# A recurrence and an FFT convolution in one kernel: filter spectra on 112 partitions, projection groups of five rows, merged products, and a new written order

## The chip, the cores and the metric

The kernel runs on one core of a Trainium2 chip. The metric is the time of one execution on the device in microseconds, given as the median of several runs. A profile is one further execution, recorded instruction by instruction; its span is the time from the program's first to its last instruction.

## The reference

Batch 4, sequence S = 6272, width D = 256. A gated recurrence runs along the sequence; its result goes through a projection into three parts, of which the second is convolved along the whole sequence with a filter (by FFT), multiplied with the other two, and projected out.

```python
sig = 1.0 / (1.0 + np.exp(-f_logit))
f = lower_bound + (1.0 - lower_bound) * sig
for t in range(S):
    h = f[:, t] * h + (1.0 - f[:, t]) * x[:, t]
    y[:, t] = h
proj = y @ w_proj                              # 256 -> 3 * 256
x1, x2, x3 = proj[..., :D], proj[..., D:2*D], proj[..., 2*D:]
X2 = np.fft.rfft(x2, n=S, axis=1)
H = np.fft.rfft(filter_fft, n=S, axis=0)
x2_conv = np.fft.irfft(X2 * H, n=S, axis=1)
out = (x1 * x2_conv * x3) @ w_out
```

## The kernel before

S is split as 128 x 49, so that the Fourier transform becomes two steps of matrix products: 128 points on the partitions (tables D1, FT) and Q = 49 rows beside them. TB = 98 partitions hold real and imaginary parts of the 49 row frequencies. The width is handled as NEP = 128 pairs of channels, in NU = 16 units of UE = 8 pairs.

- `prepare` builds the tables and the filter's spectra: it loads the filter (`ff`), turns it (`rot`, `f2`), applies the two steps (`FF1` with copies `afs`, then `FF2` with copies `hw`), and stores each pair of units into a DRAM tile H (`hst`): 128 rows, and then 64 rows once more, so that a load can read row p and row p + 49 for partition p. Tiles of H are shared by two units.
- `hgrn(b)`: 13 chunks of 512 steps. SP loads x and f_logit into XT and FL (`load`), ACT takes the sigmoid (`sig`, L324), POOL multiplies (`u`, L326), PE turns both (`su`, L338), ACT or DVE makes the gate (`f`, L351 and L353), DVE runs the scan (`scan`, L359) into HA. The first WR = 3072 steps of each half are copied behind the end (`wrap`, L367), so that strided columns can wrap around: a copy in SBUF of 512 f16 elements, given to POOL, ACT or a DMA of SP.
- `gate(b)`: x1 and x3 projections (`x13`, L387), evacuated (`xs`) and multiplied into zt (`z`, L417 on POOL, or L408 directly on DVE).
- `spectrum(b)`: `phase_p` projects x2 for all 49 rows (L705), four rows to a group of two PSUM banks, 13 groups of which the last has one row; each group is copied into X2 (`x2`, L281 or L286), every row twice, 64 columns apart. Then for each unit `phase_f1` (first step, L718, needing every group, and copy `A` into HA) and `unit` (second step F2, L777; the product with the filter's spectrum read from Hu, either directly by DVE from PSUM, L798, or copied by ACT and multiplied by POOL, L807; inverse step I2, L817, copied to Th). `spectrum_load` fetches a unit's spectrum from H into Hu. The zero-frequency column of four units at a time goes through `mini` (L734), two small DVE products (L740) and an addition on POOL (`slot`, L782).
- `phase_o(b)`: inverse step I1 (L851), product with zt (`y`, L857), output projection (`proj`, L869), copy (`o`) and store.

Matmuls, copies and DMAs are recorded as operations of a plan, each with the engines that may run it and a cost. Nothing is scheduled when the program is built: the string ORDER gives, in one written list, every operation's place, its engine and its first PSUM bank. An operation that takes `take` banks holds them until its reader is done. All four batches are interleaved in this list: while unit after unit of batch b runs, gates of b and scans of b + 1 stand between. Extra `warm` products (L591) fill PE's stream in the beginning and at the end.

SP issues all DMAs on one queue, in the list's order; a DMA whose buffer isn't free holds those behind it.

Of the kernel before, what the change touches and what calls it, by code (L numbers as in the profile page):

```python
# [11 lines left out]
F16 = mybir.dt.float16  # L12
I32 = mybir.dt.int32
AOP = mybir.AluOpType
# [9 lines left out]
M = 128  # L24
Q = 49
TB = 98
# [10 lines left out]
UE = 8  # L37
NU = NEP // UE
MARGIN = 1.0
FS = 1.0 / 8.0  # L40
HS = 64.0 / S / FS
# [4 lines left out]
NX2 = 13  # L46
# [13 lines left out]
class Plan:  # L60
# [68 lines left out]
    "YAKAEiCFCgEjKEkYEmGEnOCpQCqACwUCrYAIACjQCxME3AE4YCkAEtSAJAEuKEvKExWFLgCuUGHgEyGEzOCvECyYCsQFMgFDAFEYE5UE6ME7ME9S"
    "CtAE+CFVgE/KEwYC5WE8YC6GCzQC0AC+WFNAFFUFIQFWgFfgFggFGMC2gC/GFJIDASC3WFOYDBCFHMC4GC7YDCYFXAFYYDHSC8WFKIFPUFQMFSQF"  # L130
    "pgFqgFRMC9GDICDDWDJSFTAFUIFZUFaMDEGDKCDLYFbMDOWFhAFiYFcQFzgF0gDPGFdAFeIDQSDRCDSYDZWDMUDTSFjQDNMCGgFrAFsYAGgDaGDU"
    "CFkIFlICmgDeWDfGDXUDYEDbYF1AF2YALADgSDhKFmWF9gF+gFnOFoODcUDdEFtQFuAFvIDpSCFgFwUDnWDqCDjSFxEFyMAMAE0YDiYEEYEcYEoY"
    "DoGDrYF/AGAYF3QF4IDkCFAYDuWDvOANAMegF5IDwUDxEC1gF6SF7CF8KEAYDsWEMYJbUJcVJeNMqgDyYJgQJhRGBSDtGClgJdECVgEQYJfYJiAG"
    "CKDzWJjBJkYGDKDWgGEUD3QGIgJlSJmTGFMGGMD0GD2gGtgJnKJorGJUGKED4ADVgGPWGQOGbSGcCGdUGeMGLQGMAGRSGSKGVUGWMMgAGXQGYIGZ"
    "SGaCDFgGTWGUOCWgMsAGNUGOMGhQGiIDGgGfSGgCJqWJrXD1gJvUJxMJwQJyoJzYJsGJtHJuYGjSGkCJ0RGpUGqEJ1QJ2BJ3IJ4YGuSGwqGxYGlW"
    "GmGJ5QGnUGoEJ7IJ6RDmgG/gJ+SJ/QKACGyqGzYDlgKDWKEXKBAJ8pKFGGrSKCYG2gG3UGsKGvYG7EKGvHAQHEAHRSHSCG5sKIVJ9YG8YKKFG6YG"
    "0WHCoKJRHDYG4YHBYHFYHXSHJUHYKG1GKLBHTWHUGG9QG+AHKYHVSHWCHGWHHGKNQKORMrgMtYJpYHIgHNsHOYHLsHMYKPAKHYKQBM2gM4AHZSHa"
    "KHcUKMYHdYHlWHnGHbgMfgKRYHesHfYHgsHhYHPSHmYHQCHkgHoYHtgKSQKTRKVJKXUKUAKZMHpuHqYH/VIAFHiSHjCIDQHuUIEAHvYIBWICGHrS"
    "HsCMhYHysHzYH3QH4YIFWIGGH2gKWYHwsHxYH0UH1EIKSH5oH6YH7oH8YIJgIHWIIOIMCINYILYIOqKYQKaoKbYITUISgIPYIVEIcRIeBH9WH+GI"
    "UYIXsIbgKcUKdTKeEKfrM3gItQIuAIQWIRGIWYKhUKiVKkFIdYIfYIkgKjMI3gMiQMjAIgpIhYKlYMkIIlWIpGIYYMmUMnEMoMNDgIZSIqYImYIa"  # L140
    "CM5YKmXKoHIiQIjAInuIoYIxSIyCMuUMvMMwMIvQIwAIzWI0GKnSKrTKtDI4QKpqNCgJAgI6oI7YI1UI2MI8AI9YJJgI5YMyWNOgMzGM0OJBSJDC"
    "NPgKqYNEANFYKsRKupJSgKwQKyAIrUJEYIsEKxSJFqJGYM6WM7GKzqM+QNagNbgM8OM/ANAIKgYI+UJLYI/EJCYK1TK2SK3DK0YK4qK5YNQANGUN"
    "RYNKWNmgNngNHEK6TNIMK8DNLGJTQJXAJVANMOJHSJUYJWYJICJKUNcAK7RJMsJNYK/QK9pK+YLBAJOsJPYNSSNTCLAWNUKLCGNdYLDYKvYLEULG"
    "ENWQNwgNxgNXALFXLJWLHvJQUNYINoANpYJRELKSLOTLPXLQDLRvNBgLSYNeUNiQN7gN6gLLGNfELMqJYYNgMNjANyANzYLTTLUWLYSLaCNkILVD"
    "LWuLXYLZXLbvLcYNqUNrENsMLIYLNYNtSOEgOFgNVANuCNvKJZQNhYJaAR7WR9GMpgR8XLdQLeIR+HN0ULiSLjKN8AN9YN1EN2MN3WOOgOPgN4GN"
    "5ONNYNZALfQLgALhgLkSLnULoMLlCN+QLmgN/AOAISAWSBXSCGNlYLsSLtKSDHOGAOHYOBUOYgOZgOCEODMLxWOQAORYLpQLyOLqALrgLuSLvCLw"
    "gL2UL3MOIQOJAOKIOLWOMGONOOigOjgLzSL0COSUL7QL8IOaAObYM9YNJYL1gOVSU+gOWCOXKMlAOTEOUMMxAL4WL5GL6gU/gL9QL+AL/gOkAOlY"
    "MASMBKMFWMGOOcUOdEOeMOfQVLgVKgOgAOhIMCSMDCMEgMHWM1YOmUOnEOpSOqCOoMOrKVWgMKQMLIMPUMQMMIGMJgO6SO7KO8WO9GPCQPDAO4UO"
    "5EO+SO/KPEQVAAVXgPFAVBYO0WO1GOuUOvEOyQOzIOwSOxKVMAVNYOsUOtMVYAO2QO3IPAWPBGMMSMNCMUUMVMPKQPLIVZYPGWPHGMRSMOgMSCMZ"
    "UMaMR/YSEYPQWPUuPVYPIQPJAPMUPNEMTgPSuPTYSFSSHKSGTSIDSJYMWQPOUPPMPZYPRYMXAPYWPogPauPbYPcuPdYPpSPrCPgUPkESKQSMAPWR"  # L150
    "PhYPlYPisPjYPXBPzVP0FP7gSLQSPXSRHSNoPeRPqYPtqPuYPsYSQUSUQSWIPfBPxWPyGSVVSXtSYYSSESTYP3SP4KP1QP2APmWP8UPnGQAsQBYP"
    "vQP5SP6KQGYP9YPwAP+sP/YQFWQHGQEgQIYQJuQKYSZVQNgSbFQfQQgAQXSQOVSaUQSFSeQSgAScsSdYQbKMYgQWgQCWQPYQTYQDGQQtQRYSfRSj"
    "QShpSiYSkTSlAQpgSmDQhWQiGQLUQYYQcYSnYQZqQaYQMEQjQQkAQUWQVGSOYQqUQygQusQvYSoSSqCQlQQmAQssQtYSpTQ7gQdWQeGSrrSsYStS"
    "SvCQnQQoIQrYQ0YQzUREgQ3EQ4YQ1sQ2YRFWRJGRHGRNSROKQwQQ9YQxAQ8UQ+ERAsRBYQ/YRXgVCWVDGRPQRQAVEOVGSVjgVigRggQ5URGYRIYR"
    "KYVHCVIKQ6ERpgVOQRCWVPAVQIRDGRRURSESuSSyTS0DSwqSxYRYWSzQRauRbYS1oS2YS3RS5BRcuRdYS4SRTUS8TS+LS6CS7YS9QVSRVvgVugRU"
    "ERVURWMRZYRygRLWRiYS/ATAYVTBVUJTBQRMGVkAVlYRhURjsRkYRlsRmYVaWVbGTDAReSRrYVcORfCTCRTGUTIETHQRqSRuqRvYTEBTFYVeUV7g"
    "V6gVmWTJATKYVFgVfEVgMRsCRtYVnGTLQTNATMRTQSTRTTOpTPYVoOVqUWHgWGgVwATSCTTrTUYVrEVsMRnQR0YVxYVJgRoATVSTWWTaXTXCTcHT"
# [36 lines left out]
def kernel(  # L194
# [753 lines left out]
```

## Time and profile before

| | |
|---|---|
| Time, median of 3 runs | 463.48 us (462.63 to 464.62) |
| Span of the profiled execution | 460.2 us |
| Around the span, by the median | 3.3 us |
| Granted TensorE clock, mean | 0.996 |
| DMA | 121.40 MB, mean 264 GB/s |

The page does not give a time of the profiled execution beside its span; 3.3 us is the difference to the median. Spans and starts are in microseconds from the first instruction. Groups of instructions are told by line, engine, operation, output and inputs, shapes and count, then busy time and the mean time of one in ns, then the idle time of the engine before them with what ended it. A line can be that of a helper: L281, L283, L286, L288 and L293 are the copies of ACT (plain, scaled), DVE (plain, scaled) and POOL.

### The profile page before, as it was taken

How to read it: one execution, taken by the hardware profiler on the slowest of the kernel's cores; microseconds unless marked ns; L12 is line 12 of the kernel's file. 1: busy time of each engine (PE TensorE's matmuls, PEld its weight loads, DVE VectorE, ACT ScalarE, POOL GpSimd, SP SyncE). 2: the span in 40 equal slices, each digit the busy share in tenths (PEclk: the TensorE clock that was granted, in tenths of full speed). 3: DMA queues.
4: the chain of work that ended last, by engine and by line, in shares of the span. 5: the costliest groups of instructions: out<-in, count | busy, mean ns of one | idle time of the engine just before them, and what ended most of it. 6: DMA issues, size and time to landing. Idle time of an engine off the chain costs nothing.

```text
span 460.2 us, 14622 instructions
## 1 busy us (share of the span) xinstructions
PE 439.7 (96%) x6009; PEld 344.3 (75%) x6009; DVE 412.1 (90%) x471; ACT 402.7 (88%) x582; POOL 310.2 (67%) x293
## 2 busy tenths in 40 slices
PE   7799989999989999999999999999999999999997
PEld 5677778766756889778667889767768897777786
DVE  8689998899999996998999996999999987999872
ACT  6799988799999997899999988999998868989663
POOL 6889766188999643778898435789996603857400
PEclk9899999999999999999999999999999999999999
DMA  8967898986997997386887996579869830756176
GB/s 333 390 268 288 315 307 283 349 284 219 309 353 250 358 315 276 139 246 218 307 300 280 318 317 239 214 248 318 255 235 315 306 138 13 230 200 205 57 287 275
DMA packets 44242, 121.40 MB, mean 264 GB/s; under 512 B 4240, under 2 KB 6672, under 8 KB 44176
## 3 DMA queue, kind: packets, MB, share of 16 engines
q1 hardware_dynamic: 44176, 120.47, 74.0%
q8 instruction: 47, 0.77, 0.7%
q14 instruction: 19, 0.16, 0.1%
HBM read 87.69 MB, written 31.98 MB: 260 GB/s over the span
## 4 chain that ended last, share of the span: by engine, by line
PE 63%; DVE 12%; ACT 11%; DMA 5%; issue 5%; POOL 2%; SPq 0%; DVEq 0%; ACTq 0%; POOLq 0%
PE PS L387 14%; PE PS L817 8%; PE PS L869 7%; PE PS L338 7%; PE PS L705 6%; PE PS L777 6%; PE PS L718 5%; DVE HA L359 5%; PE PS L851 4%; DMA FL<-in_f_logit_dram 3%; DVE ys L857 2%; DVE X L286 2%; ACT FL L324 2%; PE PS L646 2%; ACT fTs L351 1%
## 5 line engine op out<-in xcount | busy, mean ns | idle before, releaser
L326 POOL TENSOR_TENSOR XT<-XT,FL 128x1024 f32<-128x1024 f32 (+1 forms) x52 | 116.9, 2251 | 50.3 <-ACT FL L324 41.9
L359 DVE TENSOR_TENSOR_SCAN HA<-fTs,HA,PS 128x512 f16<-128x512 f32 (+1 forms) x96 | 112.5, 1200 | 2.8 <-ACT fTs L351 1.7
L798 DVE TENSOR_TENSOR PP<-PS,Hu 98x1008 f16<-98x1008 f32 x87 | 101.3, 1197 | 3.4 <-ACT HA L281 1.4
L387 PE MATMUL PS<-HA,W 128*128 128x490 f16 (+1 forms) x416 | 100.4, 367 | 0.9 <-DVE X L286 0.4
L807 POOL TENSOR_TENSOR PP<-HA,Hu 98x1008 f16<-98x1008 f16 x41 | 86.2, 2107 | 1.7 <-PE PS L817 1.0
L281 ACT CAST HA<-PS 128x1024 f16<-128x1024 f32 (+1 forms) x94 | 77.0, 849 | 5.1 <-PE PS L718 3.4
L417 POOL TENSOR_TENSOR zt<-x1s,x3s 128x490 f16<-128x490 f32 (+1 forms) x43 | 52.3, 1222 | 41.8 <-ACT x3s L281 22.9
L857 DVE TENSOR_TENSOR ys<-PS,zt 128x1024 fp32r<-128x1024 f32 (+1 forms) x52 | 58.5, 1149 | 9.5 <-PE PS L851 5.0
L283 ACT ACTIVATE osb<-PS 128x1024 f32<-128x1024 f32 (+1 forms) x51 | 49.9, 992 | 13.9 <-PE PS L869 11.2
L351 ACT ACTIVATE fTs<-PS,nomc 128x512 f32<-128x512 f32 (+1 forms) x89 | 58.3, 679 | 3.7 <-PE PS L338 2.3
L387 PEld LDWEIGHTS <-W 128*128 128x128 f16 x416 | 35.4, 97 | 31.7 <-issue 5.4
L869 PE MATMUL PS<-Wo,ys 128*128 128x256 f32 x392 | 57.7, 292 | 1.3 <-DVE ys L857 1.1
L283 ACT ACTIVATE x1s<-PS 128x490 f32<-128x490 f32 (+1 forms) x92 | 53.5, 594 | 5.0 <-PE PS L387 3.0
L817 PEld LDWEIGHTS <-PP 98*128 98x128 f16 x1024 | 48.7, 98 | 10.6 <-issue 3.1
L324 ACT ACTIVATE FL<-FL 128x1024 f32<-128x1024 f32 (+1 forms) x52 | 53.0, 1026 | 2.2 <-DMA FL<-in_f_logit_dram 2.1
L869 PEld LDWEIGHTS PS<-Wo,ys 128*128 128x128 f32 x392 | 49.4, 188 | 5.8 <-DVE ys L857 2.2
L817 PE MATMUL PS<-VA,PP 98*128 98x98 f16 x512 | 52.2, 207 | 1.5 <-ACT x1s L283 0.8
L817 PE MATMUL PS<-VB,PP 98*128 98x98 f16 x512 | 51.9, 207 | 0.0
L281 ACT CAST Th<-PS 128x784 f16<-128x784 f32 x58 | 48.2, 830 | 2.6 <-PE PS L817 1.6
L338 PE MATMUL PS<-iden,FL 64*128 64x64 f32 x784 | 44.8, 230 | 1.6 <-DVE HA L359 0.9
L705 PE MATMUL PS<-W,HA 128*128 128x256 f16 x392 | 44.4, 273 | 1.0 <-ACT X L281 1.0
L705 PEld LDWEIGHTS <-HA 128*128 128x128 f16 x392 | 42.9, 142 | 1.9 <-issue 1.3
(113 smaller groups left out, 724.3 us busy)
## 6 DMA issues: line engine op xcount, KB each, us to landing
Hu<-H SPq DMA_DIRECT2D x55, 512.0 KB, 4.4
FL<-in_f_logit_dram SPq DMA_DIRECT2D x48, 512.0 KB, 5.4
XT<-in_x_dram SPq DMA_DIRECT2D x48, 512.0 KB, 5.5
out_dram<-osb SPq DMA_DIRECT2D x48, 512.0 KB, 4.3
X<-in_moe_filter_fft_dram SPq DMA_DIRECT2D x9, 512.0 KB, 7.1
H<-Hu SPq DMA_DIRECT2D x4, 512.0 KB, 6.2
Hu<-in_moe_filter_fft_dram SPq DMA_DIRECT2D x2, 512.0 KB, 9.8
H<-Hu SPq DMA_DIRECT2D x4, 256.0 KB, 6.5
```

Source lines behind the costliest of these rows:

```text
L281: nc.scalar.copy(dst, src)
L283: nc.scalar.activation(dst, src, AF.Copy, scale=scale)
L326: op("u", {"POOL": 0.1 + 0.553 * nb}, lambda e, xt=xt, ft=ft: nc.gpsimd.tensor_tensor(xt, xt, ft, op=AOP.mult), r=[("ft", k)], w=[("xt", k)])
L338: nc.tensor.transpose(bank(pb)[:, at[p] + j:at[p] + hn:nb], src[ps, j, cols], iden[ps, ps])
L359: nc.vector.tensor_tensor_scan(h, fT, bank(pb)[:, 512 - hn:512 + hn], init, op0=AOP.mult, op1=AOP.add),
L387: nc.tensor.matmul(PS[:, p, 0:n], W13[:, kh, js], HA[:, HB[kh] + t0:HB[kh] + t0 + n], start=(kh == 0), stop=(kh == 1))
L705: nc.tensor.matmul(pp[:, r - r0, :], column(HB[kh], q_of(r)), W2[:, kh, :], start=(kh == 0), stop=(kh == 1))
L798: nc.vector.tensor_tensor(pr, px.unsqueeze(1).broadcast_to([TB, 2, UE, 63]), hh, op=AOP.mult)
L807: nc.gpsimd.tensor_tensor(pr, spec[:, o, :, 1:64].unsqueeze(1).broadcast_to([TB, 2, UE, 63]), hh, op=AOP.mult)
L817: nc.tensor.matmul(PS[:, ib + o, pr * TB:(pr + 1) * TB], PP[:TB, k, o, n, 2 * pr:2 * pr + 2, :], v[:TB], start=(n == 0), stop=(n == 1))
L857: nc.vector.tensor_tensor(late["ys"][:, yk, :, 0:rn * 128], PS[:, cb:cb + 2, 0:rn * 128], late["zt"][:].rearrange("p k r m -> p k (r m)") ...
L869: nc.tensor.matmul(po[:, i, :], late["ys"][:, yk, kh, i * 128:(i + 1) * 128], Wo[:, kh, :], start=(kh == 0), stop=(kh == 1))
```

## The change

- A unit's filter spectrum is read into HP = 112 partitions instead of 128 (98 are used), and the rows that are stored a second time are HT = 48 instead of 64.
- The x2 projection has 12 groups instead of 13: the last has five rows, in three PSUM banks.
- The two small products of `mini` become one instruction over both halves.
- A wrap copy may also be given to DVE.
- ORDER is a new list, with 2422 operations instead of 2430 (four projection groups and their four copies fewer).

```diff
+HP = 112
+HT = 48
...
-NX2 = 13
+NX2 = 12
...
 ORDER = (
...
-    H = [dram.tile([2, M + 64, 2 * UE * 64], F16, name=f"H{u}") for u in range(NU // 2)]
+    H = [dram.tile([2, M + HT, 2 * UE * 64], F16, name=f"H{u}") for u in range(NU // 2)]
...
     def turned(a):
         return bass.AP(tensor=a.tensor, offset=a.offset,
-                       ap=[[a.ap[0][0], M], [Q * a.ap[0][0], 2], a.ap[1]])
+                       ap=[[a.ap[0][0], HP], [Q * a.ap[0][0], 2], a.ap[1]])
...
-                op("wrap", {"POOL": 0.05 + (z - t0) / 1015.0, "ACT": 0.08 + (z - t0) / 1200.0, "SP": 0.46},
+                op("wrap", {"POOL": 0.05 + (z - t0) / 1015.0, "ACT": 0.08 + (z - t0) / 1200.0, "SP": 0.46,
+                            "DVE": 0.07 + (z - t0) / 3840.0},
...
-            for i, (p0, n, to) in enumerate(((0, M, 0), (M - TB, 64, M)) if u % 2 else ()):
+            for i, (p0, n, to) in enumerate(((0, M, 0), (M - TB, HT, M)) if u % 2 else ()):
...
-        for g, r0 in enumerate(range(0, Q, 4)):
-            rn = min(4, Q - r0)
+        for g in range(NX2):
+            r0 = 4 * g
+            rn = Q - r0 if g == NX2 - 1 else 4
+            nb = (rn + 1) // 2
...
-            pp = op("P", {"PE": 0.005 + 0.214 * rn}, mm, r=hn + Wr(0) + Wr(1) + ["W2"], take=2)
+            pp = op("P", {"PE": 0.005 + 0.214 * rn}, mm, r=hn + Wr(0) + Wr(1) + ["W2"], take=nb)
...
         def prod(e, pb):
-            for e2 in range(2):
-                nc.vector.tensor_tensor(
-                    zp[:TB, q % 2, e2],
-                    PS[:TB, pb + e2, 0:2 * n].rearrange("p (k i) -> p k i", k=2)
-                    .unsqueeze(1).broadcast_to([TB, 2, 2, n]),
-                    Hm[:TB, e2, :, :, es], op=AOP.mult)
+            px = PS[:TB, pb:pb + 2, 0:2 * n]
+            px = bass.AP(tensor=px.tensor, offset=px.offset,
+                         ap=[px.ap[0], px.ap[1], [0, 2], [n, 2], [1, n]])
+            nc.vector.tensor_tensor(zp[:TB, q % 2], px, Hm[:TB, :, :, :, es], op=AOP.mult)
...
-            Hu[:, h].rearrange("p a e k -> p a (e k)"), turned(H[u // 2][u % 2])),
+            Hu[:HP, h].rearrange("p a e k -> p a (e k)"), turned(H[u // 2][u % 2])),
```

By engine, the two lists differ in these operations (before, after):

| operation | ACT | DVE | POOL | SP |
|---|---|---|---|---|
| x2 copies | 27, 28 | 25, 20 | | |
| wrap | 8, 4 | 0, 7 | 34, 25 | 6, 12 |
| xs copies of x1, x3 | 131, 124 | 16, 21 | | |
| x1 times x3: directly / on POOL | | 61, 63 | 43, 41 | |
| filter product: directly / on POOL | | 87, 84 | 41, 44 | |
| spectrum copies for POOL | 39, 44 | 2, 0 | | |
| A, Th, f | 202, 200 | 30, 32 | | |
| filter stage: afs, f2, hw | 57, 50 | 18, 25 | | |

More of the change, by code (lines that the diff above doesn't have):

```diff
@@ L129 @@
[L129 to L133, printed above, removed]
@@ L706, in mm @@
                                          start=(kh == 0), stop=(kh == 1))
-            pp = op("P", {"PE": 0.005 + 0.214 * rn}, mm, r=hn + Wr(0) + Wr(1) + ["W2"], take=2)
-            op("x2", either(256 * rn), lambda e, pb, r0=r0, rn=rn: copy(
+            pp = op("P", {"PE": 0.005 + 0.214 * rn}, mm, r=hn + Wr(0) + Wr(1) + ["W2"], take=nb)
+            op("x2", either(256 * rn), lambda e, pb, r0=r0, rn=rn, rows=rows: copy(
                 e, both(xv[:, :, r0:r0 + rn]),
-                PS[:, pb:pb + 2].rearrange("m a (r e) -> m (a r) e", e=256)[:, 0:rn, :]
-                .rearrange("m r (i e) -> m i e r", e=2)), w=[("x2", g)], src=pp)
+                rows(pb)[:, 0:rn, :].rearrange("m r (i e) -> m i e r", e=2)), w=[("x2", g)], src=pp)
     def phase_f1(b, u):
```

137 lines of the change are left out of this document (71 added, 66 removed).

## Prediction

> **What bounds the kernel now.** I read the page's head and its chain first, then the busy times by stage, cut at the first x2-projection matmul of each batch (75, 173, 273, 371 us) and at 445 us. Columns of the second fence: stretch, its length, busy us (instructions) of PE, PEld, DVE, ACT, POOL, granted clock, DMA share, GB/s.
>
> ```profile
> span 460.2 us, 14622 instructions
> PE 439.7 (96%) x6009; PEld 344.3 (75%) x6009; DVE 412.1 (90%) x471; ACT 402.7 (88%) x582; POOL 310.2 (67%) x293
> PE 63%; DVE 12%; ACT 11%; DMA 5%; issue 5%; POOL 2%; SPq 0%; DVEq 0%; ACTq 0%; POOLq 0%
> ```
> ```profile
> 0.00:75.00 75.00, 65.90 (x703) 50.41 (x704) 66.19 (x102) 66.00 (x99) 61.12 (x85) 0.98 0.86 313
> 75.00:173.00 98.00, 93.52 (x1373) 72.34 (x1372) 91.21 (x99) 88.86 (x129) 69.81 (x56) 1.00 0.88 304
> 173.00:273.00 100.00, 98.13 (x1440) 77.26 (x1439) 93.26 (x99) 92.32 (x134) 72.06 (x59) 1.00 0.76 267
> 273.00:371.00 98.00, 96.59 (x1416) 76.28 (x1417) 90.87 (x96) 91.10 (x135) 72.92 (x59) 1.00 0.75 263
> 371.00:445.00 74.00, 73.53 (x946) 57.73 (x941) 64.67 (x74) 58.07 (x81) 34.33 (x35) 1.00 0.45 156
> 445.00:460.20 15.20, 12.02 (x146) 10.27 (x144) 5.92 (x6) 6.39 (x7) 0.00 (x0) 1.00 0.68 270
> ```
>
> PE leads: 63% of the chain, busy 439.7 of 460.2 us. Its open time is 9.1 us before 75, 4.5 in the next stage, then 1.9, 1.4 and 0.5, and 3.2 in the tail. The change takes no matmul away, so it can only win from these 20.6 us, and from stretched matmuls that a busy PE hides. DVE and ACT stand on the chain for 12% and 11%, 55 and 51 us: a microsecond less of either's work is worth about 0.13 on the chain (55/412.1, 51/402.7). That weight is an average, and I use it where no single stage can be named. The profiled span is 460.2, the median 463.5: 3.3 us lie around the span, and I carry the difference in span over to the median.
>
> **Filter spectra: 112 partitions read, 48 rows repeated.** Rows: issues with KB and median time to landing; then pieces of the chain (start, length).
>
> ```profile
> Hu<-H SPq DMA_DIRECT2D x55, 512.0 KB, 4.4
> H<-Hu SPq DMA_DIRECT2D x4, 256.0 KB, 6.5
> ```
> ```profile
> 54.92 5.97 DMA FL<-in_f_logit_dram
> ...
> 100.43 6.23 DMA Hu<-H
> ...
> 125.69 6.87 DMA FL<-in_f_logit_dram
> ```
>
> Each of the 55 loads falls from 512 to 448 KB, 3.6 MB in all; the eight stores of repeated rows (the four shown and four alike out of other tiles) fall from 256 to 192 KB, 0.5 MB. No instruction is added on SP's queue. From 173 us on DMA is busy 0.76 and less and no DMA is among the chain's long pieces, so I cost the saving there at nothing: other transfers' slack covers it. The three long DMA pieces, 19.1 us, lie before 133, where DMA is busy 0.86 to 0.88. Sixteen of the loads and all eight stores are issued there: 1.0 + 0.5 = 1.5 MB, at 304 to 313 GB/s 4.9 us of DMA time. That is the upper bound; the lower is nothing, where a load is late because its buffer came free late. Some 37 MB move in the first 120 us, so 4% goes; transfers that queue shorten by somewhat more than the bytes: 6% of 19.1, **-1.2 us** (0 to -4.9).
>
> **x2 projection in 12 groups.**
>
> ```profile
> L705 PE MATMUL PS<-W,HA 128*128 128x256 f16 x392 | 44.4, 273 | 1.0 <-ACT X L281 1.0
> L286 DVE CAST X<-PS 128x1024 f16<-128x1024 f32 x23 | 27.3, 1220 | 12.0 <-PE PS L705 9.7 <-ACT X L281 1.6 <-DMA H<-Hu 0.6
> L281 ACT CAST X<-PS 128x1024 f16<-128x1024 f32 x25 | 25.4, 1045 | 13.4 <-PE PS L705 13.4
> L281 ACT CAST X<-PS 128x256 f16<-128x256 f32 x2 | 2.6, 1316 | 0.0
> L286 DVE CAST X<-PS 128x256 f16<-128x256 f32 x2 | 2.6, 1283 | 0.0
> ```
> ```profile
> 75.70 5.25 PE PS L705 x48
> ...
> 85.62 2.42 DVE X L286 x2
> 88.03 0.04 issue
> 88.08 0.57 PE PS L387 x2
> 88.65 0.46 PE PS L718 x8
> ```
> ```profile
> 383.77 1.30 DVE X L286
> ...
> 385.21 1.95 PE PS L718 x32
> ```
>
> The one-row copy of 256 elements is the oddity: 1.28 to 1.32 us, more than a four-row copy of 1024 (1.22 on DVE, 1.05 on ACT). It goes, four times. One four-row copy per batch becomes a five-row one, by the written order always on ACT. Its cost is not in the trace: at 1 ns per element 256 more add 0.26, so 1.3 us; if every fifth element costs what a lone one does, 1.05 + 1.32 = 2.4. I take 1.6, nearer the low end, since the fifth element follows four neighbours, as in the 1024-element row. ACT then pays 24 x 1.05 + 4 x 1.6 for 25 x 1.05 + 2 x 1.32 (+2.7), DVE 20 x 1.22 for 23 x 1.22 + 2 x 1.28 (-6.2). [...]
>
> On the path: F1 (L718) needs every group's copy. In batches 0 and 3 the lone copy came last, on the chain (the 2.42 and the 1.30). P takes 44.4/4 = 11.1 us of PE a batch, and from P's start to F1 12.95 us passed in batch 0, partly filled by x13 products. In batch 3 an ACT copy of 1.05 is now last: -0.25, and one less before it. In batch 0 the five-row copy itself is last, but eight copies stand on ACT and four on DVE instead of five and eight: DVE, which the chain followed, is relieved. I take 0.4 us in each, nothing in batches 1 and 2, whose lone copy was not last: **-0.8** (-2.6, both lone copies whole, to +1.1, the five-row copy at 2.4 and uncovered in batch 0). The group holds three PSUM banks instead of two until its copy ends; the next PE step that needs a bank waits, at most those 0.6 us.
>
> **Small products in one instruction, and work between engines.**
>
> ```profile
> L740 DVE TENSOR_TENSOR zp<-PS,X 98x128 f16<-98x128 f32 x32 | 10.5, 371 | 1.5 <-PE PS L734 1.3
> L283 ACT ACTIVATE x1s<-PS 128x490 f32<-128x490 f32 x85 | 50.0, 600 | 3.6 <-PE PS L387 3.0 <-PE PS L734 0.2
> L288 DVE TENSOR_SCALAR x1s<-PS 128x490 f32<-128x490 f32 x11 | 7.6, 694 | 0.1
> L408 DVE TENSOR_TENSOR zt<-PS,x1s 128x490 f16<-128x490 f32 x55 | 35.5, 656 | 1.6 <-ACT x1s L283 0.9 <-PE PS L387 0.2
> L281 ACT CAST HA<-PS 98x512 f16<-98x512 f32 x39 | 22.0, 603 | 1.1 <-PE PS L777 0.9
> L798 DVE TENSOR_TENSOR PP<-PS,Hu 98x1008 f16<-98x1008 f32 x87 | 101.3, 1197 | 3.4 <-ACT HA L281 1.4 <-DMA Hu<-H 1.0 <-PE PS L777 0.4
> L807 POOL TENSOR_TENSOR PP<-HA,Hu 98x1008 f16<-98x1008 f16 x41 | 86.2, 2107 | 1.7 <-PE PS L817 1.0 <-DVE zp L740 0.4 <-ACT HA L281 0.2
> L281 ACT COPY HA<-HA 128x512 f16<-128x512 f16 x8 | 5.0, 620 | 0.0
> ```
>
> Thirty-two products of 0.371 become 16 of double size. L408's 490 elements in 656 ns leave some 0.15 beside 1 ns per element, so a merged pair saves 0.15 (if the strided read sets the rest) to 0.24 (0.371 less 0.128): 2.4 to 3.8 us of DVE, I take 3.0. Counting steps by engine in both orders: 17 evacuations leave ACT, 15 of them for DVE and two for DVE's direct products (L408); five more spectra are copied by ACT (L281, 0.60), while DVE makes three direct products less (1.20) and two copies less, and POOL three more (2.1). One A copy goes from DVE to ACT. Wrap copies: ACT 8 to 4, POOL 34 to 25, DVE 0 to 7, SP's queue 6 to 12. ACT: -17 x 0.60 + 5 x 0.60 + 1.0 - 4 x 0.62 = -8.7. DVE: 15 x 0.69 + 2 x 0.66 - 3 x 1.20 - 2 x 0.69 - 1.2 - 3.0 + 7 x 0.3 = +4.6 (a wrap on DVE is not in the trace; 0.3 lies under the 0.42 that the quoted POOL-free multiply below took for as many elements). Both: -4.1 x 0.13 = **-0.5** (-1.5 to +0.8, the weights of ACT alone and DVE alone). SP's six more wraps stand ahead of later loads on its queue and may hold them; their readers, the second half's matmuls, come late, so nothing. POOL's balance, 3 x 2.1 less nine wraps, is near nought, and it is busy 67%.
>
> **New order.** PE's sequence keeps its shape: batches, interleaving and counts are the same, with x13, scans' turns and F1 shifted by a place or two. I cost that at nothing, except in the tail.
>
> ```profile
> 454.49 0.28 PE L851 MATMUL PS<-ID,Th 64*128 64x128 f16 x4
> 455.37 0.50 PE L869 MATMUL PS<-Wo,ys 128*128 128x256 f32 x2 [0.59 <-DVE ys L857]
> ```
>
> Before, the last I1 stood just ahead of the last projection, which waited 0.59 for the product between. In the new order another projection stands between the two: **-0.4** (0 to -0.6).
>
> **A wait that is added.**
>
> ```profile
> 4.64 1.02 POOL L600 CAST f<-iden 128x960 fp32r<-128x960 f32 x1
> 4.67 1.27 DVE L508 TENSOR_SCALAR PP<-HA 128x520 f32<-128x520 f32 x1
> ```
> ```profile
> 10.14 0.42 DVE L508 TENSOR_SCALAR PP<-HA 128x512 f32<-128x512 f32 x1
> ```
>
> The same line took 0.42 us with POOL still, and 1.27 when a POOL cast had begun just before: it ended 0.28 after that cast. So DVE work from SBUF to SBUF can wait out a running POOL instruction, and wraps are such work. [...] Most of the seven wraps stand beside POOL products of 2.1. Half of one, at POOL's 67%, is 0.7 us each: 4.9 of DVE, with scans, direct products and evacuations queued behind: x 0.13, **+0.6** (0 to +14.7, every wait whole and on the path).
>
> **Sum:** -1.2 - 0.8 - 0.5 - 0.4 + 0.6 = -2.3: span 457.9, median **461.2 us**, by chance on the line of 0.5% (2.3 us), which is about what a measurement can tell from no change. Its own range is 459.1 to 463.3.
>
> **Rivals.** *The order fills PE.* If the new places remove most of what PE leaves open outside the filter stage's start (4.5 + 1.9 + 1.4 + 0.5 + 3.2 = 11.5), say 40%, 4.6 more go: 456.6. For it: ACT is lighter and the copies before F1 are better divided. Against: DVE, the fuller, is not lighter outside P. *Hidden anyway.* PE's own work sets the end, loads are late by their buffers, 112 partitions land no sooner than 128, and the products were covered: 463.3. For it: 63% PE. *The wraps lose more than all the rest wins.* In the stages from 173 to 371 DVE is at 91 to 93%, and scans follow one another; a scan behind a waiting wrap is late by all of it, and so are PE's turns and the next gate. At a whole product each, 7 x 2.1 = 14.7, a little over half of it on the path gives +8 in place of +0.6: 468.6, and at 0.9 each wholly on the path 466.9; I take 467. It ends slower by over 0.5% once more than 5.2 us of waits (0.75 a wrap) are on the path.
>
> **Chances.** Forecast 0.48, half of it below 461.2; order 0.21; hidden 0.14; wraps 0.17. Faster 0.24 + 0.21 = 0.45, same 0.24 + 0.14 = 0.38, slower 0.17. The range takes in the order rival and the wraps rival with a microsecond below the one: 455.5 to 467.
>
> **What would show it.** Right: Hu<-H at 448 KB landing sooner, and shorter DMA pieces before 133; five-row copies of 1.3 to 2.4; from P's start to F1 under 12.9 and 13.8 us; zp at 0.5 to 0.6; seven DVE copies HA<-HA at 0.3, some of 1 to 2.4; ACT near 396 busy. Wrong: those copies all over 2 with scans waiting behind them; F1 waiting for the five-row copy; DMA pieces as long as before; or PE's open time after 75 changed by more than 4 us, which would make the order the cause.

## The result, and the profile after

The kernel became slower: 478.97 us (median of 4 runs, 474.88 to 479.81) against 463.92 (4 runs of the kernel before beside it), a ratio of 1.0325 [1.0272, 1.0378]. The forecast was 461.2, the range 455.5 to 467.0. Ratios here and below leave out disturbed runs (four of the ten of the variant a2, for one), so they are not always the quotient of the medians.

First the page's head and its chain, then the busy times by stage, cut as in the prediction at the first x2-projection matmul of each batch and 15 us ahead of the end.

```profile
span 477.0 us, 14612 instructions
...
PE 445.1 (93%) x6009; PEld 345.5 (72%) x6009; DVE 418.3 (88%) x468; ACT 402.9 (84%) x568; POOL 309.9 (65%) x285
...
PE 61%; DVE 17%; ACT 7%; DMA 7%; issue 6%; POOL 2%; SPq 0%; DVEq 0%; POOLq 0%; ACTq 0%
```
```profile
0.00:77.00 77.00, 64.61 (x707) 49.48 (x708) 67.54 (x107) 67.56 (x98) 58.23 (x83) 1.00 0.90 324
77.00:179.00 102.00, 96.28 (x1370) 73.34 (x1369) 88.87 (x95) 88.45 (x124) 67.30 (x53) 0.97 0.82 262
179.00:283.00 104.00, 98.68 (x1441) 77.65 (x1440) 95.29 (x98) 92.75 (x131) 71.35 (x55) 1.00 0.76 249
283.00:388.00 105.00, 99.75 (x1427) 77.30 (x1426) 98.04 (x98) 90.16 (x130) 71.93 (x55) 0.98 0.77 245
388.00:462.00 74.00, 73.59 (x943) 57.40 (x941) 62.53 (x68) 57.81 (x80) 41.07 (x40) 1.00 0.44 147
462.00:477.00 15.00, 12.23 (x133) 10.29 (x131) 6.06 (x7) 6.16 (x6) 0.00 (x0) 1.00 0.65 258
```

The stages were 75, 98, 100, 98, 74 and 15.2 us long; they are 77, 102, 104, 105, 74 and 15. Most of the loss lies in the stages in which units of one batch, its gates and the scans of the next are interleaved. The same 6009 matmuls keep PE busy 5.4 us longer (445.1 against 439.7), at a clock of 0.97 and 0.98 in two stages, and PE stands open 31.9 us instead of 20.5. The two add up to the 16.8 us between the spans.

**The wraps on DVE.** One row for all seven (least, median and longest in ns, first and last start), and the group's row; then the instructions around the longest, around the second longest, and around one that waited little.

```profile
L286 DVE COPY HA<-HA x7: 267/470/4481, 49.9 to 350.3; 128x512 f16<-128x512 f16 x7
L286 DVE COPY HA<-HA 128x512 f16<-128x512 f16 x7 | 8.7, 1240 | 0.0
```
```profile
350.27 2.10 POOL L810 TENSOR_TENSOR PP<-HA,Hu 98x1008 f16<-98x1008 f16 x1
350.34 4.48 DVE L286 COPY HA<-HA 128x512 f16<-128x512 f16 x1
...
352.33 2.34 POOL L326 TENSOR_TENSOR XT<-XT,FL 128x1024 f32<-128x1024 f32 x1
...
354.74 0.66 DVE L409 TENSOR_TENSOR zt<-PS,x1s 128x490 f16<-128x490 f32 x1
...
355.45 0.57 PE L388 MATMUL PS<-HA,W 128*128 128x490 f16 x2 [3.57 <-DVE zt L409]
```
```profile
249.31 2.37 POOL L326 TENSOR_TENSOR XT<-XT,FL 128x1024 f32<-128x1024 f32 x1
249.44 2.39 DVE L286 COPY HA<-HA 128x512 f16<-128x512 f16 x1
251.75 0.66 DVE L409 TENSOR_TENSOR zt<-PS,x1s 128x490 f16<-128x490 f32 x1
...
253.65 0.50 PE L872 MATMUL PS<-Wo,ys 128*128 128x256 f32 x2 [1.73 <-DVE HA L359]
```
```profile
144.20 4.74 POOL L326 TENSOR_TENSOR XT<-XT,FL 128x1024 f32<-128x1024 f32 x2
...
146.19 0.52 DVE L286 COPY HA<-HA 128x512 f16<-128x512 f16 x1
```

A free copy takes 0.27 us. The one at 249.44 ended 0.15 us behind the POOL instruction that had begun just before it. The one at 350.34 was not let in between two POOL instructions that followed each other without a gap: it took both, 4.48 us. That is not always so. The one at 146.19 came in between two such instructions, 0.14 us behind the end of the first (at 146.57), and so did one at 223.03 (0.47 us); what decides is not settled. Behind the copy at 350.34 on DVE stood the direct product (L409), behind that PE's next x1/x3 projection, whose bank the product held: PE stood 3.57 us. Behind the copy at 249.44 a scan came late, and PE stood 1.73 us.

**The loads.** One place in the first batch, of the kernel after (the first row is a piece of the chain, a load from its issue to its landing); then the waits for loads, of after and of before (line, releaser: us in all, times, longest).

```profile
126.12 8.28 DMA FL<-in_f_logit_dram
...
134.43 1.06 ACT L324 ACTIVATE FL<-FL 128x1024 f32<-128x1024 f32 x1 [2.95 <-DMA FL<-in_f_logit_dram]
135.39 0.80 ACT L281 CAST Th<-PS 128x784 f16<-128x784 f32 x1
...
136.24 0.69 PE L338 MATMUL PS<-iden,FL 64*128 64x64 f32 x8 [2.46 <-ACT Th L281]
```
```profile
ACT FL L324 <- DMA FL<-in_f_logit_dram: 5.4, 5, 3.0
POOL XT L326 <- DMA XT<-in_x_dram: 6.0, 4, 2.7
DVE PP L801 <- DMA Hu<-H: 2.5, 4, 1.5
```
```profile
ACT FL L324 <- DMA FL<-in_f_logit_dram: 2.1, 2, 1.2
POOL XT L326 <- DMA XT<-in_x_dram: 2.4, 3, 1.5
```

The load took 8.28 us, where the median of these loads is 5.2, and ACT waited 2.95 us for it. The copy of Th (L281) was behind that wait on ACT's queue, and the bank that it frees was what PE's next turn (L338) needed: 2.46 us. The loads are smaller and the waits for them grew: 5.4 from 2.1, 6.0 from 2.4, 2.5 from 1.0.

**The clock behind a stop.** Windows after the stops of 2.46 and 3.57 us (columns as above; the last three are granted clock, DMA share, GB/s).

```profile
136.00:142.00 6.00, 5.76 (x46) 3.42 (x46) 3.23 (x3) 5.25 (x9) 4.75 (x3) 0.50 0.95 318
142.00:146.00 4.00, 4.00 (x63) 2.60 (x63) 3.81 (x4) 2.34 (x4) 3.00 (x2) 1.00 0.21 31
...
355.40:357.00 1.60, 1.55 (x21) 1.21 (x21) 1.60 (x2) 0.83 (x2) 0.00 (x0) 1.00 0.13 44
357.00:360.40 3.40, 3.40 (x24) 1.71 (x24) 2.35 (x5) 2.08 (x4) 0.00 (x0) 0.50 0.33 113
360.40:363.00 2.60, 2.60 (x49) 2.19 (x44) 2.31 (x3) 1.85 (x4) 2.31 (x1) 1.00 0.41 99
```

In the variant a1 (below) the half clock came with a shorter stop too:

```profile
67.40 0.69 PE L337 MATMUL PS<-iden,FL 64*128 64x64 f32 x8 [1.32 <-ACT PP L282]
```
```profile
67.10:74.00 6.90, 6.60 (x50) 5.62 (x52) 4.59 (x4) 5.30 (x10) 5.78 (x9) 0.51 0.97 312
```

The granted clock was 0.50 for 6.0 us behind the one stop (it fell at 135.1, while PE still stood) and for 3.4 us behind the other (from 357.0, when PE had run for 1.5 us), and 1.00 again after that. Six products of L388 (128x490) took 2.65 us from 139.43, at 0.50, and 1.25 us from 250.67, at 1.00. If all matmuls are taken to need twice their time at half clock, which is an estimate from these six, 5.76 and 3.40 us of busy PE hold 2.9 and 1.7 us too much, 4.6 together, which is most of the 5.4. So these two stops were paid about twice. The length of a stop alone does not decide: the one of 1.73 us left the clock at 1.00 (from 250 to 264), the one of 1.32 us in a1 did not (0.51). What decides is not shown.

**Where the 16.8 us are.** The two stops behind wraps (3.57 and 1.73) and the one behind the load (2.46) are 7.8 us, most of the 8 by which PE is open longer behind the filter stage; in the kernel before, the longest stop there is 0.81 us. The half clock behind two of them is an estimated 4.6. That makes an estimated 7 us for the wraps and 5.4 for one late load. The filter stage is 1.3 us longer; the rest is in no single place.

### The profile page after: what moved, and what is told of

Read it like the earlier page. It is cut to its first block, busy times and chain, and to the rows that moved or that the text cites. A ratio compares the mean times of both kernels' runs of the same rounds, so it can differ in the third digit from the quotient of the medians.

```text
span 477.0 us, 14612 instructions
## 1 busy us (share of the span) xinstructions
PE 445.1 (93%) x6009; PEld 345.5 (72%) x6009; DVE 418.3 (88%) x468; ACT 402.9 (84%) x568; POOL 309.9 (65%) x285
## 4 chain that ended last, share of the span: by engine, by line
PE 61%; DVE 17%; ACT 7%; DMA 7%; issue 6%; POOL 2%; SPq 0%; DVEq 0%; POOLq 0%; ACTq 0%
PE PS L388 15%; PE PS L711 9%; PE PS L820 8%; DVE HA L359 7%; PE PS L872 5%; PE PS L723 5%; PE PS L338 5%; PE PS L780 5%; DMA FL<-in_f_logit_dram 4%; DVE ys L860 4%; PE PS L854 3%; PE PS L647 2%; DVE PP L801 1%; PE PS L665 1%; ACT fTs L351 1%
## 5 line engine op out<-in xcount | busy, mean ns | idle before, releaser
L388 PE MATMUL PS<-HA,W 128*128 128x490 f16 (+1 forms) x416 | 105.3, 375 | 6.3 <-DVE zt L409 3.9
L801 DVE TENSOR_TENSOR PP<-PS,Hu 98x1008 f16<-98x1008 f32 x84 | 98.3, 1199 | 3.7 <-DMA Hu<-H 2.5
L810 POOL TENSOR_TENSOR PP<-HA,Hu 98x1008 f16<-98x1008 f16 x44 | 92.4, 2106 | 9.8 <-DVE zp L747 5.5
L281 ACT CAST HA<-PS 128x1024 f16<-128x1024 f32 (+1 forms) x100 | 80.0, 832 | 6.9 <-PE PS L723 2.7
L418 POOL TENSOR_TENSOR zt<-x1s,x3s 128x490 f16<-128x490 f32 (+1 forms) x41 | 50.0, 1225 | 41.1 <-ACT x3s L281 18.5
L351 ACT ACTIVATE fTs<-PS,nomc 128x512 f32<-128x512 f32 (+1 forms) x88 | 57.6, 672 | 7.0 <-PE PS L338 5.5
L388 PEld LDWEIGHTS <-W 128*128 128x128 f16 x416 | 35.6, 99 | 37.4 <-issue 14.2
L283 ACT ACTIVATE x1s<-PS 128x490 f32<-128x490 f32 (+1 forms) x89 | 50.8, 582 | 10.1 <-DVE zt L409 4.4
L324 ACT ACTIVATE FL<-FL 128x1024 f32<-128x1024 f32 (+1 forms) x52 | 52.4, 1012 | 5.6 <-DMA FL<-in_f_logit_dram 5.4
L820 PE MATMUL PS<-VB,PP 98*128 98x98 f16 x512 | 52.4, 208 | 0.0
L281 ACT CAST Th<-PS 128x784 f16<-128x784 f32 x56 | 45.9, 819 | 6.3 <-PE PS L820 5.7
L338 PE MATMUL PS<-iden,FL 64*128 64x64 f32 x784 | 45.2, 231 | 5.3 <-ACT Th L281 2.5
L338 PEld LDWEIGHTS PS<-iden,FL 64*128 64x128 f32 x784 | 34.0, 139 | 19.8 <-DVE HA L359 5.5
```

What stands on the lines that cost most here:

```text
L281: nc.scalar.copy(dst, src)
L283: nc.scalar.activation(dst, src, AF.Copy, scale=scale)
L338: nc.tensor.transpose(bank(pb)[:, at[p] + j:at[p] + hn:nb], src[ps, j, cols], iden[ps, ps])
L388: nc.tensor.matmul(PS[:, p, 0:n], W13[:, kh, js], HA[:, HB[kh] + t0:HB[kh] + t0 + n], start=(kh == 0), stop=(kh == 1))
L801: nc.vector.tensor_tensor(pr, px.unsqueeze(1).broadcast_to([TB, 2, UE, 63]), hh, op=AOP.mult)
L810: nc.gpsimd.tensor_tensor(pr, spec[:, o, :, 1:64].unsqueeze(1).broadcast_to([TB, 2, UE, 63]), hh, op=AOP.mult)
```

## The experiments

In the expectations W stands for the seven wraps on DVE, S for the sequence of the transfers on SP's queue, C for the places and engines of the computing steps. "Old list" and "new list" are ORDER before and after. The table collects the stage lengths of one profiled execution of each, as differences to the kernel before (75.5 us filter stage; 52.4 the four projection stages P; 59.9, 59.3, 57.6, 47.6 the unit stages U0 to U3, from the first F1 of a batch to its first I1; 107.7 the output stages O). The borders are taken from PE's instructions.

| kernel | ratio to before, interval | span | filter | P | U0 | U1 | U2 | U3 | O |
|---|---|---|---|---|---|---|---|---|---|
| after | 1.0325 [1.0272, 1.0378] | 477.0 | +1.3 | -1.8 | +5.0 | +4.4 | +6.9 | +1.0 | +0.1 |
| a1_wraps_act | 1.0175 [1.0136, 1.0214] | 473.1 | +3.8 | -1.7 | +3.4 | +2.4 | +3.8 | +1.0 | +0.2 |
| a2_wraps_before | 1.0126 [1.0077, 1.0174] | 468.1 | +1.4 | -1.8 | +1.7 | +2.8 | +2.9 | +1.0 | -0.2 |
| b4_before_dve_wraps | 1.0089 [1.0045, 1.0132] | 462.9 | -0.6 | +0.2 | -1.4 | +1.5 | 0.0 | 0.0 | +2.9 |
| c1_edits_old_order | 1.0087 [1.0053, 1.0120] | 463.7 | -0.6 | +4.3 | -1.2 | 0.0 | +0.4 | 0.0 | +0.5 |
| c2_edits_old_order_new_p | 1.0124 [1.0075, 1.0173] | 470.5 | +2.4 | +5.8 | +0.6 | +0.5 | +0.6 | +0.1 | +0.4 |
| d1_before_spectra_and_product | 1.0047 [1.0016, 1.0077] | 460.7 | -1.0 | 0.0 | +0.2 | -0.1 | +0.3 | 0.0 | +1.0 |
| a3_old_dma_sequence | 1.0484 [1.0399, 1.0568] | 486.8 | -0.5 | +6.2 | +12.2 | +2.8 | +3.0 | +1.6 | +1.3 |
| c5_new_dma_sequence | 1.0221 [1.0133, 1.0308] | 469.6 | +1.2 | +3.8 | -0.3 | +1.3 | +2.7 | 0.0 | +0.6 |
| s1_before_no_stores | 0.9960 [0.9923, 0.9996] | 460.2 | -0.1 | 0.0 | +1.3 | 0.0 | +0.2 | 0.0 | -1.4 |
| s2_new_list_no_stores | 1.0116 [1.0046, 1.0186] | 464.6 | +1.4 | -1.7 | +1.8 | +1.5 | +1.6 | +1.0 | -1.2 |
| e2_new_order_old_engines | 1.0651 [1.0569, 1.0732] | 495.0 | +6.8 | -1.3 | +9.4 | +6.7 | +4.8 | +4.6 | +3.8 |
| z1_half_small_product | 1.0166 [1.0128, 1.0205] | 469.4 | 0.0 | -1.8 | +2.0 | +2.3 | +6.2 | +0.5 | 0.0 |
| h1c_new_filter_stage | 1.0744 [1.0675, 1.0814] | 497.2 | +2.4 | +5.6 | +26.4 | +0.3 | +0.5 | 0.0 | +1.8 |

A stage of one execution moves by some three microseconds where nothing in it was changed: the filter stage, the same in c1 and c2, gives -0.6 and +2.4, and U2 is +6.2 in z1 and +2.9 in a2. The verdicts rest on the ratios, and the columns tell where to look.

**What the wraps cost.** In the first two the new list stays, and only the wraps' engines change; in the third the old list gets the new wraps.

```diff
 # a1: new list
-wrap DVE x7
+wrap ACT x7
 # a2: new list, all 48 wraps on the old list's engines
-wrap ACT x4, DVE x7, POOL x25, SP x12
+wrap ACT x8, POOL x34, SP x6
 # b4: old list, the same seven wraps
-wrap ACT x8, POOL x34, SP x6
+wrap ACT x7, DVE x7, POOL x29, SP x5
```

> The changed kernel with its seven DVE wrap copies given to ACT at the same places of the list; nothing else differs. Theory W (a DVE copy from SBUF to SBUF waits until POOL is still between two instructions, and the rest queues behind it): the two copies that took 4.48 and 2.39 us go, with the 3.6 and 1.7 us that the TensorE stood still behind them: 5 to 7 us less than the changed kernel, 472 to 474, and ACT copies of 0.62 with no wait. Theory O (the new list is bad elsewhere too, loads issued late): 6 of the 15 us at most come back, some 9 stay. Theory E (the edits themselves, 112 partitions, five-row copies): nothing comes back, 479.

Measured: 473.12 us, ratio 1.0175. That is in W's range, and it leaves the 9 us of O as well.

> The changed kernel with each of its 48 wrap copies on the engine that the kernel before gives it (34 POOL, 8 ACT, 6 DMA), at the places of the new list. W: like the run with ACT, 472 to 474. A rival, D: the six added wrap DMAs on SP's queue hold the loads of f_logit behind them (one such load was waited for 3.0 us); then this one is faster than the ACT variant by 2 us or more, 469 to 471. O: no better than the ACT variant. E: 479.

Measured: 471.8 us, ratio 1.0126, between W's range and D's. Its interval overlaps with that of a1, so D is not shown.

> The kernel before with only the seven wrap copies (by batch and place in the chain of chunks) that the changed kernel gives to DVE given to DVE. W: each copy beside POOL work takes 0.3 to 4.5 us instead of 0.27; on average 1.2 as in the changed kernel, and the time grows by 2 to 8 us, 466 to 472. Rival: DVE has room for them and it stays at 463 to 465.

Measured: 466.49 us, ratio 1.0089, at the low end of W's range. Its seven copies:

```profile
L283 DVE COPY HA<-HA 128x512 f16<-128x512 f16 x7 | 4.3, 621 | 0.0
```

Taking the copies off DVE gives back 1.5% (a1), 7 us of the 15, and putting every wrap back, those of SP too, 2.0% (a2), 9 us. In the old list the same copies cost 0.9%, with 4.3 us of DVE instead of 8.7. The pages of a1 and a2 have these lines for PE:

```profile
PE 444.7 (94%) x6009; PEld 346.8 (73%) x6009; DVE 410.8 (87%) x461; ACT 406.0 (86%) x575; POOL 309.4 (65%) x285
```
```profile
PE 440.2 (94%) x6009; PEld 342.9 (73%) x6009; DVE 410.8 (88%) x461; ACT 403.8 (86%) x572; POOL 313.4 (67%) x294
```

PE of a2 is open 27.9 us: of the 8.9 us between the spans of after and a2, 4.9 are slow matmuls and 4.0 open time, and what is left of a2's loss is open time. a1 is open 28.4 us and has slow matmuls too, so these don't come with the wraps alone.

**The edits under the old list.** c1 makes every edit and keeps the old list, with the five-row group where the one-row group stood; c2 gives c1 the new list's sequence, engines and banks in the projection stages; d1 makes only the spectra's 112 and 48 rows and the merged product.

```diff
 # c1: all edits; ORDER of before, without its 13th projection groups
-P take=2, x2   (12th group, four rows)
...
-P take=2, x2   (13th group, one row)
+P take=3, x2   (12th group, five rows, copied by ACT)
 # d1: before with
+HP = 112
+HT = 48
+ one tensor_tensor in mini
```

> All edits (112 and 48 rows, 12 groups, merged products) with the list of the kernel before: the five-row group stands where the one-row group stood, on ACT, and the other last group's place is dropped; wraps are as in the kernel before, none on DVE. O and W (order and wraps carry the loss): 461 to 464, the kernel before or 1 to 2 us under it. E: 470 or more.

Measured: 467.91 us, ratio 1.0087, between the two ranges.

> All edits, the list of the kernel before and its wraps, but within the projection stages the groups in the changed kernel's sequence, engines and banks. The hand-placed five-row groups of the first variant lost 0.7, 1.5 and 2.1 us from the projection's start to F1 in batches 1 to 3, where the changed kernel gains 0.6, 0.3 and 0.5. If the loss of that variant lies there alone: 4 to 5 us under it, 459 to 463 on this chip's scale of 463 for before. If the edits cost elsewhere: 465 or more.

Measured: 467.71 us, ratio 1.0124. It did not mend the projection stages.

> The kernel before, its list unchanged (13 groups), with 112 and 48 rows and the merged product only. The first variant with all edits was 1.8 us ahead of before at the end of batch 0's unit stage and lost 4.3 later in the projection stages; without the five-row groups that loss goes: 460 to 463, at or 1 to 3 us under before. If it is over before by more than 2, the two edits cost by themselves.

Measured: 465.97 us, ratio 1.0047. Less work was moved and computed, and the kernel was not faster. It is 2 to 3 us over before, so by the mark set ahead the two edits cost something by themselves; how is not settled.

Under the old list the unit stages keep their length (c1: -1.2, 0, +0.4, 0), so the loss of after in U0 to U2 is not a cost that these edits have by themselves. c1 loses in the projection stages, where PE waits for copies to free its banks (PE's waits of c1, then of before):

```profile
PE PS L710 <- ACT X L280: 2.6, 2, 1.5
...
PE PS L710 <- DVE X L285: 1.5, 3, 0.6
```
```profile
PE PS L705 <- ACT X L281: 1.0, 2, 0.5
```

**The transfers.** a3 is a2 with SP's DMAs in the old list's sequence, c5 is c1 with them in the new list's. s1 and s2 store 8 of the 128 partitions of the output, in the kernel before and in a2.

```diff
 # a3, c5: only the order of the DMAs among themselves
-load, H, store, wrap in this list's sequence
+load, H, store, wrap in the other list's sequence
 # s1, s2
-out[b].rearrange(...)[:, r0:r0 + rn, :], late["osb"][k][:, 0:rn, :]
+out[b].rearrange(...)[0:8, r0:r0 + rn, :], late["osb"][k][0:8, 0:rn, :]
```

> The changed kernel with the wraps' engines of the kernel before (the variant that was 8 to 9 us over before), and its 251 DMAs issued by SP in the sequence of the kernel before (six of them moved where a reader came first). Theory S (the new sequence of DMAs lets loads of spectra and of x land late: the slowest tenth of spectrum loads took 7.5 us against 6.1): most of those 8 us go, 464 to 467. Theory C (the new places of DVE, ACT and POOL work make the TensorE wait): it stays at 470 to 473.

Measured: 487.17 us, ratio 1.0484.

> All edits with the list of the kernel before (the first such variant, 467.9) and its wraps, but its DMAs in the changed kernel's sequence. S: 5 to 8 us slower than that variant, 472 to 476, with spectrum loads landing later. C: within 2 us of it.

Measured: 476.93 us, ratio 1.0221.

> The kernel before, storing only 8 of 128 partitions of each output piece (the rest of the output is left unwritten): 24 of 121 MB less on the DMA engines. Together with the next run this separates late transfers from other waits. Here, 1 to 4 us under before: 460 to 462.

Measured: 461.28 us, ratio 0.996.

> The changed kernel with the wraps' engines of the kernel before (8 to 9 us over before), with the same cut of the stores. Theory D (the new list loses by transfers that land late, its slowest tenth of spectrum loads at 7.5 us): with a fifth of the traffic gone the loss to the run above shrinks to 3 us or less. Theory C (places of DVE, ACT and POOL work): the loss stays at 6 to 9 us.

Measured: 468.39 us, ratio 1.0116.

Neither sequence is the better one: each loses under the other's computing steps, 3.6% and 1.3% more than its own partner (a3 against a2, c5 against c1). a3 came out above both ranges. c5 came out just above S's range, and as S had it its spectrum loads landed later, at a median of 4.5 us against 4.2 in c1. In a3 most of the loss in U0 are three waits of PE for POOL's small addition (`slot`); the rows are these waits in the window 88 to 162, three pieces of the chain, and the matmul:

```profile
PE PS L819 <- POOL PP L784: 9.8, 3, 5.9
```
```profile
112.48 5.91 DMA XT<-in_x_dram
...
120.81 2.34 POOL XT L325
123.15 0.30 POOL PP L784
```
```profile
123.50 0.26 PE L819 MATMUL PS<-VA,PP 98*128 98x98 f16 x1 [5.89 <-POOL PP L784]
```

The addition takes 0.30 us, but it stands on POOL's queue behind two multiplies, and the first of them waits for x.

With nearly no stores the new list still loses 1.6% to the old one (1.0116 against 0.996), 7 us as theory C had it, and no less than with them. In the profiles U1 and U2 lose 1.5 and 1.6 instead of 2.8 and 2.9, and the stops of PE that stand behind late loads in a2 (see the account below) are no longer among PE's largest waits, of 1.2 us and more, but the ratios don't bear out that relief. So late transfers are not shown to carry the whole rest.

**Engines, order, filter stage.** e1 is c1 with each unit operation on the new list's engine, e2 is a2 with each on the old list's. 109 operations differ. z1 halves the merged product in a2. h1 puts the new list's filter stage ahead of c1's rest, h2 the old one's ahead of a2's rest; h1b, h2b and h1c are the same with other banks.

```diff
 # e1, e2: engines only
-fr, afs, f2, hw, f, xs, A, Th, prod, o on this list's engines
+the same on the other list's engines
 # z1
-nc.vector.tensor_tensor(zp[:TB, q % 2], px, Hm[:TB, :, :, :, es], op=AOP.mult)
+na = 2 if b == 0 and q < 2 else 1
+nc.vector.tensor_tensor(zp[:TB, q % 2, :, 0:na], px[:, :, 0:na], Hm[:TB, :, 0:na, :, es], op=AOP.mult)
 # h1, h2: operations ahead of the first P of batch 0
-filter stage of this list
+filter stage of the other list
```

> The new list's order with the seven wraps on the old engines as in a2_wraps_before (471.8 us), and every other unit operation on the engine that the old list gave it. If the engines carry the loss: 465 to 468, with U1 and U2 within 1 us of the kernel before. If the order carries it: 470.5 to 474, with U1 and U2 longer by 2 to 4 us. By the two together, if each is fitted to the other: above 474.

Measured: 493.48 us, ratio 1.0651. That is the third case: the new order without its engines loses another 5%.

> All edits, the instructions in the old list's order as in c1_edits_old_order (467.9 us), but each unit operation on the engine that the new list gives it (109 differ; wraps and projection evictions keep theirs). If the engines of the new list carry what is left of its loss (a2_wraps_before: 471.8): 472 to 477, with the gain of the unit stages in c1 (U0 -1.2) turned into losses. If the order carries it: 466.5 to 469.5, as c1. I hold the order for likelier, 0.6 to 0.4.

Measured: 527.79 us, ratio 1.1382. In this kernel the results of 22 matmul groups are overwritten before the list reads them, so part of the output comes from other data and some waits are not those of the order; I read from it only that it is far from 472 to 477.

> a2_wraps_before (471.8 us), with the merged small product halved: from the third product of batch 0 on it writes one of its two repeated parts, 128 elements instead of 256, so that it takes about 0.34 us, the cost that the list was made with, instead of 0.595; the other part keeps its first values. If the list's loss comes from this product being longer than its cost says, on the path of the first passes that wait for it: 469 or less, with U1 and U2 shorter by 1 to 2 us each. If it comes from the places of the large operations: 471 to 472.

Measured: 471.08 us, ratio 1.0166. The product fell as meant, to 0.368 us, and the time did not: that the list counted this product at 0.34 us and it takes 0.595 is not the cause.

> The new list's filter stage (everything ahead of the first projection matmul of batch 0), then the rest of the old list as in c1_edits_old_order (467.9). If the filter stage's order by itself costs: +1.4 us there (76.8 instead of 75.5) and the units as in c1, so 469 to 470. If not: 467 to 468.5.

Measured: 480.41 us, ratio 1.0365.

> The old list's filter stage, then the rest of the new list with its wraps as in a2_wraps_before (471.8). If the filter stage carries 2 us of the loss: 469 to 470. If the unit stages carry all: 471 to 473. If the loads that the new filter stage issues early are what the new unit stages need: above 473.

Measured: 475.13 us, ratio 1.0251.

> h1_new_filter_stage with the banks of 19 matmul groups exchanged so that each group's reader is ahead of the next writer. The stall of 8.5 us in U0 of the first form should be gone: about 472. If the new filter stage by itself is what loses: prep +1 to +3 and the rest as in c1_edits_old_order, 469 to 471; if the old unit stages lose where another filter stage stands ahead of them: U0 +2 or more, 471 to 474.

Measured: 482.67 us, ratio 1.0453.

> h2_old_filter_stage (475.1) with one projection group's banks mended. 474 to 476: the old filter stage ahead of the new unit stages costs 3 to 4 us more than the new one, so it is not the filter stage's order that carries the new list's loss.

Measured: 476.18 us, ratio 1.028.

In h1 one copy and in h2 two read another bank than their matmul wrote, and in h1b and h2b the readers of the 19 and the two groups with new banks do; that part of the output is made from other values.

> h1_new_filter_stage with 19 matmul groups on other banks and every reader on its group's bank: the new list's filter stage, then the old list's order as in c1_edits_old_order (467.9 us). If the new filter stage only loses its own 1 to 3 us and the old unit stages run as they did: 469 to 471, U0 within 1 us of the kernel before. If the old unit stages need the old filter stage ahead of them: U0 longer by 2 us or more, 471 to 476.

Measured: 496.58 us, ratio 1.0744. U0 is 26.4 us longer; from 95 to 125 us PE is busy for 16.5 us of the 30, at a clock of 0.69.

h1c was meant to tell what the new filter stage costs the old units and doesn't: 23 steps of U0 were moved to where their banks are free, and PE waits among them. h1, h1b and h1c lie above all that I had expected. h2 and h2b, the new units behind the old filter stage, are slower than a2, so the old filter stage does not win a2's loss back; as part of their data is other and their border is new, they don't show more.

No version with the whole computation was faster than the kernel before.

## Why the prediction was wrong

**Two steps failed: the weight of 0.13 on the added wait, which made it +0.6, and "New order... I cost that at nothing".** On DVE the seven wraps cost 7 us more than on ACT (a1). Without them the new list is still 1.3% over before (a2), 6 us where the rest of the sum had -2.9.

**The new order.** The 1.3% are not the list's alone, for the edits cost 0.9% under the old list (c1). But c1 loses in the projection stages, and there a2 gains 1.8 us; its U0 to U2 lose 7.4 in that profile and its filter stage 1.4. My reason was that PE's sequence keeps its shape. It does: 702 of the 758 PE operations that both lists have stand within two places of where they stood. But PE waits for steps of ACT, DVE and POOL, and those I had only counted by engine. PE's waits behind the filter stage, of a2 and then of before:

```profile
PE PS L337 <- ACT Th L280: 1.7, 1, 1.7
PE PS L387 <- DVE PP L800: 1.6, 2, 1.4
PE PS L722 <- DVE PP L800: 1.3, 1, 1.3
```
```profile
PE PS L387 <- DVE PP L798: 0.3, 1, 0.3
```

The three are 4.6 us, and PE of a2 is open 4.1 us longer than before behind the filter stage. Two of them pass on a late load. The direct product ahead of x13 waited for a spectrum (a piece of the chain, then two instructions):

```profile
226.80 7.61 DMA Hu<-H
```
```profile
234.50 1.21 DVE L800 TENSOR_TENSOR PP<-PS,Hu 98x1008 f16<-98x1008 f32 x1 [1.64 <-DMA Hu<-H]
235.76 0.57 PE L387 MATMUL PS<-HA,W 128*128 128x490 f16 x2 [1.38 <-DVE PP L800]
```

Th stood on ACT's queue behind a sigmoid that waited 1.88 us for f_logit, though a scan on the chain would have held it nearly as long. Ahead of F1 two direct products follow each other, and no load is waited for: a step of the same length as before, in a place where PE needs it. In the sum the places stood at nothing, and loads that land later did not stand at all. Why the loads land later under the new list, and what would have to change to win the rest back, stays open. The experiments speak against the merged product as its carrier (z1), don't settle the filter stage's part (PE of a2 is open 3.3 us longer there), and show that the order without its engines, or with the other list's transfers, is slower still.

**The added wait: right mechanism, wrong weight.** The copies took 8.7 us instead of 7 x 0.3 = 2.1: 6.6 us of waits, above the 4.9 that I took and the 5.2 from which the rival decides. But I put 0.13 on them, the average share of DVE on the chain. Two copies made nearly all of it, and each stopped DVE's queue with steps behind it that PE needed: some 7 us for 6.6 us of waits, a weight of about one, 1.7 of it by the half clock. The rival "the wraps lose more", at 467, was the nearest; it had no price for the clock, nor for the list.

**DMA, -1.2: not seen.** The loads are 448 KB and land in 4.2 us instead of 4.4, but the slowest tenth took 7.7 us and more, against 6.2 before, and DMA's pieces of the chain rose from 5% to 7%:

```profile
Hu<-H SPq DMA_DIRECT2D x55, 448.0 KB, 4.2
```

Under the old list, too, the saving does not show (d1, 1.0047). That queued transfers shorten by 6% where 4% of the bytes go was my estimate; no run shows it. For this edit and the merged product the rival "hidden anyway" came nearest.

**12 groups, -0.8: -1.8 in the new list, +4.3 under the old one.** The mechanism was right where the list was made for it, and the copy cost what I took:

```profile
L281 ACT CAST X<-PS 128x1280 f16<-128x1280 f32 x4 | 6.3, 1584 | 0.4 <-PE PS L711 0.2
```

1.58 us against 1.6. What I missed is that the group costs more in a list that was not made for it (c1); that its third bank, which I put at "at most 0.6 us", does it is likely by PE's waits there, but not shown by itself.

**Merged product, ACT and DVE.** The product took 0.595, forecast 0.5 to 0.6, and saves 1.0 us of DVE in all instead of 3.0:

```profile
L747 DVE TENSOR_TENSOR zp<-PS,X 98x256 f16<-98x256 f32 x16 | 9.5, 595 | 1.0 <-PE PS L739 1.0
```

DVE rose by 6.2 us, of which the waiting copies alone are 6.6; ACT is at 402.9, not near 396, and neither sum set the time: single places did. The range of this term was wrong, too: -8.7 and +4.6 at 0.13 are -1.1 and +0.6, not -1.5 and +0.8.

**The tail, -0.4: not seen.** The last projection no longer waits, but the one that now stands ahead of it waits 0.52 us for its product, where 0.59 were to go; the output stages are as long as before (+0.1).

**The test that I had named** does not tell what I thought. PE's open time after 75 us changed by more than 4 us (to 19.5, from 11.5), which "would make the order the cause"; but 5.3 of the 8 us are the two stops behind wraps.

## What to carry over

A written list is fitted to itself: engines, places, banks and transfers (the other list's engines cost another 5%, e2 against a2; its transfers 3.6% and 1.3%, a3 and c5). Costing a new one by what each engine has to do in sum says little; follow for some PE waits which step is released last and whether that step waits for a load, and ask where the new list puts both. A wait that can stand in front of a queue has the weight of what is queued behind it (here some 7 us for 6.6 us of waits), not the engine's average weight on the chain (0.13). And less work under an unchanged list need not be faster (d1, 1.0047).

## What the hardware showed that I had not expected

A DVE copy from SBUF to SBUF waited not for one POOL instruction but for two that followed each other (4.48 us against 0.27 free), while two other copies got in between two such instructions (0.52 and 0.47 us). The copy that took 2.39 us ended 0.15 us behind the one POOL instruction beside it; the end of the first of the two beside the copy of 4.48 us did not let that one in. And stops of PE of 1.32, 2.46 and 3.57 us went with 6.9, 6.0 and 3.4 us at half clock, one of 1.73 us with none.
